# Larger fill transfers, a folded last batch, halved last copies and key transposes by DMA, with a new order, in an attention and gated-convolution kernel

## The chip, the cores and the metric

The kernel runs on one core of one Trainium2 chip. The metric is the device time of one execution in microseconds (us). Before the change it is 197.87 us (median of three runs, 197.86 to 203.43).

TensorE is called PE here, VectorE DVE, ScalarE ACT, GpSimd POOL and SyncE SP, as in the profile. Transfers issued by SP and ACT go by hardware queues ("hardware transfers"), those issued by POOL by the software queue.

## The reference

```python
# q, k, v: (8 batches, 8 heads, 576, 64); p: (8, 8, 32, 64); all float32
p_packed = softmax_attention(p, k, v)            # 32 packed queries per head
a = softmax_attention(q, p_packed, p_packed)     # 576 queries over 32 packed keys
x = a.transpose(0, 2, 1, 3).reshape(8, 576, 512)
x1, x2, x3 = split(x @ w_proj, 3)                # w_proj: (512, 1536)
X2 = rfft(x2, axis=1)
conv = irfft(X2 * rfft(filter, axis=0), axis=1)  # filter: (576, 512)
out = (x1 * conv * x3) @ w_out                   # (8, 576, 512)
```

The Fourier transforms are matrix products with constants: `wc` and `wt` go to the spectrum, `ac` comes back. `filter` is transformed once, in the fill (products `hp`). Per batch, keys and queries are transposed (`kTp`, `qTp`), scored (`s1`, `s2`), and so on to the output products `o`.

## The kernel before

All operations are recorded first, then put in an order by a built-in plan and emitted in that order, engine by engine. Each batch's keys, values and queries come by three software transfers. Cuts are marked with `...`.

```python
# every tile of the working pools; bufs is the number of buffers of a tag
def tile(self, pool, shape, dtype, tag, bufs, name, kind=None):
    t = pool.tile(shape, dtype, tag=tag, name=name, bufs=bufs)
    self.slot[t.tensor.name] = ((tag, bufs), kind) if kind else ((tag, bufs),)
    return t
...
# the plan counts how many buffers of a tag are in use, not which ones
if any(used[tag] + held.get(tag, 0) + n > limit[tag] for tag, n in more.items()):
...
def load(b):
    ...
    qn = sb([P, H, 4 * D], FP16, tag="qn", name=f"qn_b{b}")          # bufs=2
    nc.gpsimd.dma_start(kn[:], ...)
    nc.gpsimd.dma_start(vn[:], ...)
    nc.gpsimd.dma_start(qn[:], ...)
    ...
    if b >= TURNED:                                                    # 4
        nc.sync.dma_start_transpose(qT..., qn...)                      # queries by DMA
...
# the fill
nc.sync.dma_start(ident[:], d_id.ap()[:])
for i in range(4):
    nc.scalar.dma_start(wc[:, i, :], d_wc.ap()[:, i, :])
    nc.sync.dma_start(filt[i][:], fsrc[:, TILE_I[i], :])
nc.scalar.dma_start(wt[:], d_wt.ap()[:])
nc.sync.dma_start(filt[4][0:32, :], ftail[0])
nc.sync.dma_start(filt[4][32:64, :], ftail[1])
load(0)
...                                                                    # wp, three parts
nc.sync.dma_start(ac[:], d_ac.ap()[:])
load(1)
...
# keys, all batches: PE transposes into PSUM, copies by DVE or ACT
nc.tensor.transpose(tp[:, hh, ii, :], kn[:, 2 * g + hh, ts(ii, P)], ident[0:KP, 0:KP])
...
pair, APART = [None], (0, B - 1)      # batches whose inverse products are not folded
...
os_ = sb([P, DM], FP32, tag="os", name=f"os_b{b}", bufs=5)
nc.scalar.mul(out=os_[:], in_=o[:], mul=float(1.0 / SC_Y))
```

The softmax here doesn't subtract the row's maximum and nothing guards it: scores larger than these inputs give would overflow.

## Time and profile before

| | before |
|---|---|
| fast runs / slow runs seen | about 197.8 to 199.8 / 203 to 206 us |
| profiled span | 195.3 us, granted clock 1.00 |
| PE busy | 183.8 us, 94% of the span |
| chain that ended last | PE 87%, DMA 6% |
| first real matmul | 7.77 us |
| last matmul ends | 190.5 us |

PE decides. The fast runs are of two sorts: 197.8 to 198.0 us where the granted clock was 0.999 or 1.00, 198.6 to 199.8 where it was 0.984 to 0.991. "Loss", which the prediction defines, is the time at which a matmul starts less the useful matmul work before it: where loss is flat PE is fed, and each step up is a stop. The lines themselves stand in the prediction.

### The profile page before, as it was taken

How to read it: one execution, taken by the hardware profiler on the slowest of the kernel's cores; microseconds unless marked ns; L12 is line 12 of the kernel's file. 1: busy time of each engine (PE TensorE's matmuls, PEld its weight loads, DVE VectorE, ACT ScalarE, POOL GpSimd, SP SyncE). 2: the span in 40 equal slices, each digit the busy share in tenths (PEclk: the TensorE clock that was granted, in tenths of full speed). 3: DMA queues.
4: the chain of work that ended last, by engine and by line, in shares of the span. 5: the costliest groups of instructions: out<-in, count | busy, mean ns of one | idle time of the engine just before them, and what ended most of it. 6: DMA issues, size and time to landing. Idle time of an engine off the chain costs nothing.

```text
span 195.3 us, 5806 instructions
## 1 busy us (share of the span) xinstructions
PE 183.8 (94%) x2425; PEld 116.2 (59%) x2425; DVE 143.9 (74%) x268; ACT 126.3 (65%) x265; POOL 133.3 (68%) x108
## 2 busy tenths in 40 slices
PE   5949979999999999999999999999999999999990
PEld 4614745676775677656666666667656565664640
DVE  4435575988759987988798699848698897796720
ACT  0634586777998989847686775888667935434241
POOL 7611547697466999679987999399159968963100
PEclk9999999999999999999999999999999999999999
DMA  6999999999999999999999695934012202322335
GB/s 173 242 293 193 206 208 196 197 202 204 191 189 269 202 217 140 112 203 221 141 286 172 148 229 60 203 146 111 0 54 78 90 0 82 138 55 107 110 103 166
DMA packets 44842, 30.95 MB, mean 158 GB/s; under 512 B 16336, under 2 KB 39376, under 8 KB 44816
## 3 DMA queue, kind: packets, MB, share of 16 engines
q0 software_dynamic: 29312, 16.52, 61.2%
q1 hardware_dynamic: 14784, 13.34, 27.4%
q10 hardware_dynamic: 720, 0.72, 1.4%
q8 instruction: 19, 0.31, 0.6%
q14 instruction: 7, 0.06, 0.1%
HBM read 35.55 MB, written 9.44 MB: 230 GB/s over the span
## 4 chain that ended last, share of the span: by engine, by line
PE 87%; DMA 6%; ACT 2%; POOL 1%; issue 1%; DVE 0%; SPq 0%; ACTq 0%
PE x_b L493 31%; PE o_b L493 16%; PE f_b L493 9%; PE fp_b L493 5%; PE s_b L493 5%; PE kTp_b L493 4%; PE qp_b L493 4%; DMA ident<-c_id 3%; PE pv_b L493 3%; PE hp L493 3%; DMA filt<-in_moe_filter_fft_dram 3%; PE a2tp_b L493 2%; PE qTp_b L493 1%; PE fpt_b L493 1%; POOL a_b L493 1%; ACT e_b L493 1%
## 5 line engine op out<-in xcount | busy, mean ns | idle before, releaser
L493 PE MATMUL x_b<-a2t_b,qm_b 128*128 128x64 f16 (+1 forms) x256 | 47.0, 286 | 0.0
L493 POOL TENSOR_TENSOR gm_b<-tt_b,tt_b 128x512 f16<-128x512 f32 (+1 forms) x28 | 39.3, 1427 | 7.3 <-DVE tt_b L493 6.8
L493 DVE TENSOR_TENSOR tt_b<-f_b,h 128x1024 f32<-128x1024 f32 x32 | 38.4, 1218 | 5.5 <-PE f_b L493 5.3
L493 PE MATMUL x_b<-ac,gm_b 128*128 128x64 f16 (+3 forms) x312 | 41.0, 252 | 0.0
L493 PE MATMUL o_b<-wout,y_b 128*128 128x512 f16 x128 | 37.9, 379 | 0.0
L493 POOL TENSOR_TENSOR tt_b<-tt_b,tt_b 128x1024 f32<-128x1024 f32 x12 | 28.3, 2360 | 10.1 <-DVE tt_b L493 9.2
L493 ACT ACTIVATE os_b<-o_b 128x512 f32<-128x512 f32 x36 | 21.3, 598 | 19.6 <-PE o_b L493 18.8
L493 DVE TENSOR_TENSOR w_b<-x1s_b,x_b 128x512 f32<-128x512 f32 (+1 forms) x40 | 24.8, 628 | 8.4 <-ACT x1s_b L493 5.0
L493 PEld LDWEIGHTS <-gm_b 128*128 128x128 f16 x312 | 23.7, 98 | 11.2 <-issue 1.3
L493 ACT COPY x1s_b<-x_b 128x512 f32<-128x512 f32 (+1 forms) x40 | 21.6, 548 | 10.5 <-PE x_b L493 6.0
L493 ACT CAST qm_b<-qp_b 128x512 f16<-128x512 f32 x48 | 26.0, 598 | 2.9 <-PE qp_b L493 1.6
L493 ACT ACTIVATE e_b<-s_b 96x384 f16<-96x384 f32 (+1 forms) x48 | 23.7, 526 | 3.7 <-PE s_b L493 2.6
L493 PE MATMUL f_b<-qm_b,fa_b 128*128 128x512 f16 x80 | 25.9, 380 | 0.0
L493 POOL TENSOR_TENSOR fa_b<-ez_b 128x512 f16<-128x512 f32 x14 | 17.7, 1273 | 9.5 <-ACT ez_b L493 9.5
L493 POOL TENSOR_TENSOR a_b<-e_b,zr_b 128x1152 f16<-128x1152 f16 (+2 forms) x10 | 17.3, 1739 | 9.1 <-DVE zr_b L493 5.1
L493 DVE SCALAR_TENSOR_TENSOR y_b<-w_b,x_b 128x512 f16<-128x512 f32 x32 | 21.1, 683 | 2.6 <-PE x_b L493 2.4
L493 PEld LDWEIGHTS <-qm_b 128*128 128x128 f16 x256 | 18.1, 98 | 8.0 <-issue 0.6
L493 PEld LDWEIGHTS <-a_b 128*128 128x128 f16 x240 | 17.1, 98 | 8.8 <-POOL a_b L493 2.3
L493 PEld LDWEIGHTS <-y_b 128*128 128x128 f16 x128 | 11.3, 98 | 7.8 <-issue 0.2
L493 ACT COPY ez_b<-fp_b 128x512 f32<-128x512 f32 x16 | 9.4, 590 | 8.9 <-PE fp_b L493 4.6
L493 PE MATMUL kTp_b<-ident,kn_b 96*128 96x96 f16 x192 | 14.2, 206 | 0.0
L493 PEld LDWEIGHTS <-kn_b 96*128 96x128 f16 x192 | 11.2, 97 | 2.6 <-issue 0.2
(78 smaller groups left out, 300.5 us busy)
## 6 DMA issues: line engine op xcount, KB each, us to landing
out_dram<-os_b SPq DMA_DIRECT2D x24, 256.0 KB, 2.4
kn_b<-in_k_dram POOLq DMA_DIRECT2D x8, 576.0 KB, 10.8
vn_b<-in_v_dram POOLq DMA_DIRECT2D x8, 576.0 KB, 13.6
qn_b<-in_q_dram POOLq DMA_DIRECT2D x8, 512.0 KB, 12.1
out_dram<-os_b SPq DMA_DIRECT2D x16, 128.0 KB, 2.4
wp<-in_moe_w_proj_dram POOLq DMA_DIRECT2D x3, 512.0 KB, 16.4
filt<-in_moe_filter_fft_dram SPq DMA_DIRECT2D x4, 256.0 KB, 5.5
out_dram<-os_b SPq DMA_DIRECT2D x16, 64.0 KB, 2.3
```

Source lines behind the costliest of these rows:

```text
L493: ins = op.call(*op.args, **op.kw).ins
```

## The change

The intent: take PE work away (keys of batches 6 and 7 transposed by DMA; batch 7 folded), shorten the fill (eight hardware transfers, so that none waits for another), shorten the end (last copies in halves on two engines), and plan the order anew.

```diff
-    kTr = [... for r in range(4)]
+    kTr = [... for r in range(5)]
-    TURNED = 4
+    TURNED, KEYS, NK = (4, 5, 6, 7), (6, 7), 5
...
-    nc.sync.dma_start(ident[:], d_id.ap()[:])
-    for i in range(4):
-        nc.scalar.dma_start(wc[:, i, :], d_wc.ap()[:, i, :])
-        nc.sync.dma_start(filt[i][:], fsrc[:, TILE_I[i], :])
-    nc.scalar.dma_start(wt[:], d_wt.ap()[:])
...
+    half = slice(0, 768), slice(768, 1664)                   # wc with the identity at its end
+    for u in range(2):
+        nc.scalar.dma_start(wci[:, half[u]], d_wc.ap()[:, half[u]])
+        nc.sync.dma_start(filt[:, ts(u, 2 * DM)], fsrc[:, ts(u, 2 * DM)])
+    for u in range(2):
+        nc.scalar.dma_start(wt[64 * u:64 * u + 64, u, :], ...)
+        nc.vector.memset(wt[64 * u:64 * u + 64, 1 - u, :], 0.0)
+        nc.sync.dma_start(ftail[32 * u:32 * u + 32, :], fend[u])
...
-    nc.sync.dma_start(ac[:], d_ac.ap()[:])
+    nc.gpsimd.dma_start(ac..., d_ac...)
...
+        if b in KEYS:
+            for g in range(4):
+                nc.sync.dma_start_transpose(kTr[(4 * b + g) % NK]..., kn[:, 2 * g:2 * g + 2, :]...)
...
+            by = nc.vector if b == 0 else nc.gpsimd          # normalisation of batch 0
...
-    pair, APART = [None], (0, B - 1)
+    APART = (0,)
...
+            if b == B - 1:
+                nc.scalar.mul(out=os_[:, 0:DM // 2], ...)
+                nc.vector.tensor_scalar_mul(out=os_[:, DM // 2:], ...)
...
-PRIORITY = (...)                                             # the order, a packed table
+PRIORITY = (...)
```

Smaller changes are left out here (fewer buffers for `pk` and `zs`, the filter in another tile, the model of transfers inside the plan).

## The prediction

> **What bounds the kernel now.** I read first how busy each engine is in stretches of the span, then the chain that ended last, then the timeline of the fill and of the end, and the groups by shape for durations. Columns of the first view: stretch, its length, then busy microseconds (us) per engine with the number of instructions, granted TensorE clock, DMA share, GB/s.
>
> ```profile
> 0.00:5.00 5.00, 2.88 (x14) 2.08 (x15) 2.28 (x13) 0.01 (x1) 3.94 (x9) 1.00 0.62 174
> 5.00:10.00 5.00, 5.00 (x25) 2.93 (x24) 1.98 (x3) 3.02 (x4) 3.02 (x5) 1.00 1.21 246
> 10.00:15.00 5.00, 2.50 (x12) 0.74 (x11) 1.83 (x4) 1.75 (x4) 0.74 (x1) 1.00 1.18 285
> ...
> 40.00:60.00 20.00, 20.00 (x376) 13.99 (x371) 14.42 (x35) 16.21 (x37) 14.31 (x14) 1.00 1.49 200
> ...
> 120.00:140.00 20.00, 20.00 (x298) 12.98 (x295) 16.15 (x32) 14.91 (x35) 13.97 (x10) 1.00 0.63 125
> ...
> 190.00:195.30 5.30, 0.49 (x3) 0.00 (x0) 0.00 (x0) 0.90 (x2) 0.00 (x0) 1.00 0.60 187
> ```
>
> From 40 us to 190 PE, the first engine, is busy all the time and no other engine is over 93% in any stretch. Before that and after it, it isn't. Busy can hide small gaps, because a 512-column matmul lasts 0.38 us while the next starts after 0.216. So I summed each matmul's issue time instead (columns/2.4 + 2.5 ns, not below 27 ns; the 4- or 8-fold overlapped small ones divided accordingly; fillers named spin count nothing). Call the time minus this useful work done so far the **loss**. In the trace the loss is 7.8 us when the first real matmul starts (7.77), 11.4 at the first key transpose (17.95), 12.7 at 21.8, 14.3 at 25.2, 16.8 at 29.2 and 17.55 at 32.4. From there to the last matmul at 190.5 it grows by only 2.1, nearly all at the changes of tile shape around the qp and pv products. So the kernel is: 17.5 us lost in the fill, 170.6 us of PE work, 2.1 us of switching, 4.8 us after the last matmul.
>
> The chain that ended last (start, length, what) shows what the fill waits for:
>
> ```profile
> 1.20 5.18 DMA filt<-in_moe_filter_fft_dram
> 6.39 0.35 SPq L493
> ...
> 6.78 6.26 DMA ident<-c_id
> 13.04 0.14 issue
> 13.18 0.22 PE pTp_b L493
> 13.39 4.72 PE hp L493 x18
> 18.11 1.02 PE kTp_b L493 x24
> ...
> 185.65 0.69 PE o_b L493 x3
> ```
>
> The identity is the eleventh transfer on the two hardware queues; SP issues it only when an earlier one has landed, because eight are allowed at once (its instruction waits for that count). So no transpose can start before 13.0, and the filter products (hp) come so late that they keep PE till 18. The POOL timeline gives the landings of the other stream, since each issue waits for an earlier transfer:
>
> ```profile
> 12.80 0.74 POOL L493 DMA_DIRECT2D wp<-in_moe_w_proj_dram  x1 [3.91 <-DMA kn_b<-in_k_dram]
> 17.31 0.79 POOL L493 DMA_DIRECT2D kn_b<-in_k_dram  x1 [3.77 <-DMA vn_b<-in_v_dram]
> 19.93 0.63 POOL L493 DMA_DIRECT2D qt_b<-in_q_dram  x1 [1.83 <-DMA qn_b<-in_q_dram]
> ```
>
> Keys at about 12.5, values 17.0, queries 19.6; later landings in the trace are 2.6 to 3.5 us apart. Values took 4.5 us because the constant ac (576 KB) was under way beside them.
>
> **The Trainium skill.** "TensorE: Matmul & The Clock Gate", section "Back-to-back issue gap", gives N/2.4 + 2.5 ns between matmuls at full clock. The trace agrees: 24 key transposes of 96 columns in 1.02 us are 42.5 ns each, the formula says 42.5. "DMA: Bandwidth & Descriptors", "Rules for kernel authors", says to coalesce small transfers into large ones and that issuing from several engines does not add bandwidth, since all use the same 16 DMA engines. The trace agrees with the second part (values slow beside ac) and cannot show the first. The same page, "Latency and other measured facts", gives 261 GB/s for a DMA transpose; here the 512 KB query transposes take 7.2 us from issue to landing, about 73 GB/s, so I use 7.2 and a quarter of the bytes per key piece, about 3 us. None of the pages says when a transfer on a hardware queue is delayed by the software queue.
>
> **Part by part.**
> 1. *Keys of batches 6 and 7.* Removed: 2 x 24 PE transposes at 42.5 ns = 2.04 us, all on the bound engine, plus 4 copies of 644 ns on ACT and 4 of 448 ns on DVE, which lie beside PE. Added: eight transposes on SP's queue. In the new order batch 6's keys can be transposed from 84 us of PE work on and are used at 94; batch 7's between 100 and about 108, used from 113 to 117. There is room, and the DMA share at that stage is low (0.63 and less).
> 2. *Batch 7 folded.* Each of four inverse products has 3 x 512, 2 x 288 and 2 x 224 columns before, 3 x 288 and 3 x 224 after: 3 x 215.8 less 122.5 and 95.8 = 429 ns, four times 1.72 us; the 64-column ones go from 20 to 12, 8 x 29.2 ns = 0.23. Together 1.95 us of PE. Added on POOL: two sums of 2.36 us become two sums and four of 1.27, 5.1 us more, in the last 50 us, where POOL is under half busy.
> 3. *The fill.* Eight hardware transfers, none waiting for another; identity within the first constants; half of wt is cleared on chip and not loaded; ac goes behind the second batch on the software queue. About 1.73 MB must land for the filter products. At the 230 to 250 GB/s of this stage, from about 2 us, that is 9 to 9.5 us, against 12.3 before. The activation table loads at about 2.5 instead of 5.0, since ACT no longer waits to issue. I estimate the first hp at 6.0 (the first half is 0.7 MB), a wait for the second half to about 9.5, and the first key transpose, which comes after 5.67 us of work in the new order, at 12.6: loss 6.9, not 11.4. The rest of the chain added 6.1 us of loss; DVE instead of POOL for batch 0's normalisation takes up to 0.5 off. That makes 12.5 to 13.
>    The other limit is the software stream. With keys at 10.5 and the old distances: values 13.6, queries 16.4, first two parts of wp 19.6 and 22.6, keys of batch 1 25.7, last wp 28.4, values 31.4, queries 34.3, ac 36.6, keys of batch 2 39.5. The new order needs them after 14.9, 17.9, 21.4, 22.9, 24.3 and 28.0 us of work (from keys of batch 1 on), so the loss is at least 10.8, 10.5, 10.0, 11.4, 12.3 and 11.5. Both limits nearly meet; I take 13.2 instead of 17.55: **4.3 us** gained.
> 4. *The end.* Timeline, last line:
>
> ```profile
> 190.57 0.60 ACT L493 ACTIVATE os_b<-o_b 128x512 f32<-128x512 f32 x1 [0.27 <-PE o_b L493]
> ```
>    Halves of 256 columns on ACT and DVE should take about 0.38 us (the 256-column copies here take 381 and 418 ns), so 0.2 us less; one issue beside another on the second queue may give 0.1 more. 0.3 us.
>
> Sum: 2.04 + 1.95 + 4.3 + 0.3 = 8.6 us. I take off 0.8 for new waits, below. 197.87 - 7.8 = 190.1, rounded to 190.0.
>
> **Rivals.**
> - *The folded batch makes POOL the end.* PE has 11.6 us of work between the last spectrum product of batch 7 and its first inverse. POOL needs batch 6's four sums first, then 2 x 2.36 + 4 x 1.27. Reckoned from the spectrum product, the first folded sum has 1 to 2 us of slack and the fourth about none. If POOL or DVE runs late, PE idles 1 to 3 us: 191 to 193. For it: the loss before is flat (19.6) from 155 to 187 us, so nothing hid this; against: the order was made for it.
> - *SP blocks.* Its queue is in order: the transposes of batch 7 wait until the score products of batch 6 have released the key buffers, and five finished output tiles stand behind them. All five buffers are then full, and ACT's next output copy, at 107 us of work, could wait 2 to 3 us for a store to land, stopping ACT. PE's PSUM buffers cover part: 0 to 2 us, 190 to 192.
> - *The fill is limited by bandwidth and hardly moves.* All bytes but 160 KB still come; if larger transfers run no faster and the stream of batch 1 lands only 1.5 us earlier, loss goes to 16: 192.8. Against: ac is out of the way of keys, values and queries.
> - *Fill better than thought:* loss 11.5, 188.4.
>
> **Range and chances.** PE's 4 us are near certain, as PE is the bound for 150 us. The fill gives 2 to 6, new waits take 0 to 3. So 187.6 to 192.8 eight times in ten. 2% is 193.9; missing it needs a poor fill and a late POOL together. Faster 0.94, within 2% 0.05, slower 0.01.
>
> **What would show it.** Identity no longer in the chain; first hp near 6 us, first kTp near 12.6; PE loss near 13 at 33 us and about 15 at the end; PE matmuls 48 + 12 fewer besides spins; kTp x144 instead of x192; x_b at 512 columns from ac x12. Wrong if PE shows gaps over 0.5 us after 33 us, especially before the last inverse products (released by POOL gm_b), or near the SP transposes (ACT os_b released by a DMA), or if keys of batch 0 land no earlier than 12.

## The result

The changed kernel takes **205.61 us** (median of four runs, 204.26 to 206.62), against 200.65 us for the kernel before in the same rounds (197.86 to 203.65). Ratios here are the mean time of one kernel's fast runs over that of the other's of the same rounds, so not quite the ratio of the medians: 1.039, interval 1.028 to 1.049. The prediction said 190.0 and 0.94 for faster. It was slower.

The busy-time view by stretch (length; PE, PE weight load, DVE, ACT, POOL with instruction counts; granted clock; DMA share; GB/s) of the changed kernel:

```profile
5.00:10.00 5.00, 3.89 (x17) 1.62 (x16) 1.90 (x3) 2.27 (x4) 2.36 (x3) 1.00 1.20 279
10.00:15.00 5.00, 4.83 (x38) 2.06 (x37) 3.31 (x8) 2.31 (x5) 2.27 (x3) 1.00 1.41 197
40.00:60.00 20.00, 20.00 (x338) 13.51 (x336) 14.42 (x32) 17.68 (x40) 14.20 (x14) 1.00 1.41 210
60.00:70.00 10.00, 10.00 (x208) 7.62 (x206) 9.29 (x20) 9.33 (x22) 3.48 (x3) 1.00 1.51 214
70.00:80.00 10.00, 0.53 (x9) 0.26 (x5) 1.24 (x3) 0.93 (x3) 1.24 (x2) 0.73 0.81 127
80.00:85.00 5.00, 1.73 (x14) 0.75 (x22) 0.00 (x0) 0.58 (x1) 5.00 (x4) 0.50 0.84 105
85.00:90.00 5.00, 5.00 (x53) 2.58 (x54) 4.33 (x5) 2.93 (x6) 5.00 (x5) 0.68 0.55 105
90.00:95.00 5.00, 5.00 (x121) 3.84 (x118) 4.04 (x6) 3.08 (x7) 5.00 (x4) 1.00 0.01 3
```

The fill is better: PE is busy for 4.83 of the 5 us from 10 to 15, where it had 2.50. Then, from 70 to 80, PE is busy for 0.53 us of 10, and DVE, ACT and POOL for no more than 1.24 each; POOL comes back first, at 78.7. The same view in finer stretches shows a clock of 1.00 up to 74.5, 0.50 from there to 88.2, and 1.00 again after it. "TensorE: Matmul & The Clock Gate" in the Trainium skill, section "What's actually happening", says that the clock drops to half after an idle window of about 3.4 us and comes back after a busy one. The trace agrees: PE's last matmul before the stop ends at 70.5, the clock drops 4.0 us later, and it comes back 4.9 us after PE's restart at 83.3 (the 0.73 and 0.68 above are means over a stretch).

Loss tells how much each cost. It is 15.1 us at 69.4, 28.1 at 83.3 and 30.4 at 90, against 18.3 in the kernel before from 69 to 80. So one stop of 12.9 us and 2.3 us of cold clock lie in these 20 us. From 90 to the last matmul loss grows by only 1.7. Take the 15.2 us away from 205.6 and 190.4 is left, which is about what was predicted; the repaired kernel of experiment 1 will take 1.7 us more than that. The question is what the stop is.

The chain that ended last, for the changed kernel (start, length, what), runs straight through it:

```profile
55.49 17.80 DMA qn_b<-in_q_dram
73.44 4.74 DMA qT_b<-qn_b
...
78.75 0.89 POOL qn_b L509
79.66 2.35 POOL tt_b L509
82.00 1.23 POOL fa_b L509
83.28 0.61 PE f_b L509
```

Before, the chain was PE from 13 us on, but for DVE, ACT and POOL between 23 and 30. Here a load (17.8 us from issue to landing), a DMA transpose, and then three POOL instructions come first. The POOL timeline of the changed kernel says which instruction stood there, and for how long:

```profile
63.14 0.82 POOL L509 DMA_DIRECT2D kn_b<-in_k_dram  x1
78.74 0.89 POOL L509 DMA_DIRECT2D qn_b<-in_q_dram  x1 [14.78 <-DMA qT_b<-qn_b]
79.66 2.35 POOL L509 TENSOR_TENSOR tt_b<-tt_b,tt_b 128x1024 f32<-128x1024 f32 x1
81.96 1.26 POOL L509 TENSOR_TENSOR fa_b<-ez_b 128x512 f16<-128x512 f32 x1
```

And the PE timeline, at the end of its stop:

```profile
83.28 0.61 PE L509 MATMUL f_b<-qm_b,fa_b 128*128 128x512 f16 x1 [12.74 <-POOL fa_b L509]
```

POOL was ready to issue the load of batch 5's queries at 64 us. It waited 14.8 us, until the transpose of batch *4's* queries had landed. The sum `fa` of batch 2, which PE needed at 70.5, stood two instructions behind on the same queue.

In the kernel before, the same load comes after those sums (its issue is at 77.75 us, without a wait):

```profile
74.07 2.52 POOL L493 TENSOR_TENSOR gm_b<-tt_b,tt_b 128x512 f16<-128x512 f32 x2
76.53 1.29 POOL L493 TENSOR_TENSOR fa_b<-ez_b 128x512 f16<-128x512 f32 x1
77.75 0.91 POOL L493 DMA_DIRECT2D qn_b<-in_q_dram  x1
```

Why should loading batch 5 wait for a transpose of batch 4? The addresses of the query tiles in the two built kernels say it. By batch, 0 to 7, the buffer is

```
before   0 1 0 1 0 1 0 1
changed  0 1 0 1 0 0 1 0
```

Batch 5's queries were given the buffer that batch 4's had just been given. Batch 3's buffer was as good as free (in experiment 1 a load into it waits 0.9 us); why the pool did not hand it out was not looked into. The load must therefore wait until batch 4's queries have been loaded *and* read. Of all tiles with two buffers per batch, only the queries have this break in the alternation. The built instruction list of the changed kernel (which could be read before predicting) shows both halves of the trouble:

```
46 kn_b_330 <- in_k_dram                       [waits for a load, PE]
47 qn_b_332 <- in_q_dram                       [waits for DMAHW6 (the transpose), two loads]
48 tt_b_310 <- tt_b_299, tt_b_310
49 fa_b_293 <- ez_b_295
```

### The profile page after: what moved, and what is told of

The parts are those of the page before. It is cut to its first block, busy times and chain, and to the rows that moved or that the text cites.

```text
span 204.0 us, 5677 instructions
## 1 busy us (share of the span) xinstructions
PE 179.8 (88%) x2353; PEld 112.3 (55%) x2353; DVE 145.3 (71%) x272; ACT 122.9 (60%) x261; POOL 137.5 (67%) x111
## 3 DMA queue, kind: packets, MB, share of 16 engines
q1 hardware_dynamic: 18944, 13.70, 28.1%
## 4 chain that ended last, share of the span: by engine, by line
PE 56%; DMA 22%; POOL 12%; DVE 5%; issue 2%; ACT 1%; SPq 1%; POOLq 0%; ACTq 0%
PE x_b L509 19%; PE o_b L509 12%; DMA qn_b<-in_q_dram 9%; DMA vn_b<-in_v_dram 7%; PE f_b L509 6%; DMA ftail<-in_moe_filter_fft_dram 4%; PE fp_b L509 3%; POOL tt_b L509 3%; POOL gm_b L509 3%; POOL fa_b L509 3%; PE hp L509 3%; PE s_b L509 2%; DMA qT_b<-qn_b 2%; PE qp_b L509 2%; PE pv_b L509 2%; DVE tt_b L509 2%
## 5 line engine op out<-in xcount | busy, mean ns | idle before, releaser
L509 PE MATMUL x_b<-a2t_b,qm_b 128*128 128x512 f16 (+1 forms) x256 | 45.4, 287 | 0.6 <-DVE tt_b L509 0.6
L509 POOL TENSOR_TENSOR tt_b<-tt_b,tt_b 128x1024 f32<-128x1024 f32 x14 | 33.0, 2361 | 6.6 <-DVE tt_b L509 6.5
L509 PE MATMUL f_b<-qm_b,fa_b 128*128 128x512 f16 x80 | 25.9, 392 | 12.7 <-POOL fa_b L509 12.7
L509 PE MATMUL x_b<-ac,gm_b 128*128 128x64 f16 (+3 forms) x300 | 35.8, 252 | 0.4 <-DVE y_b L509 0.2
L509 PE MATMUL o_b<-wout,y_b 128*128 128x512 f16 x128 | 35.8, 379 | 0.0
L509 ACT ACTIVATE os_b<-o_b 128x512 f32<-128x512 f32 (+1 forms) x36 | 20.2, 570 | 12.4 <-PE o_b L509 11.4
L509 PEld LDWEIGHTS <-qm_b 128*128 128x128 f16 x256 | 17.8, 98 | 10.1 <-issue 1.1
L509 POOL TENSOR_TENSOR fa_b<-ez_b 128x512 f16<-128x512 f32 x15 | 19.0, 1277 | 4.0 <-ACT ez_b L509 3.9
L509 POOL DMA_DIRECT2D qn_b<-in_q_dram x8 | 7.3, 912 | 16.7 <-DMA qT_b<-qn_b 14.8
L509 POOL TENSOR_TENSOR a_b<-e_b,zr_b 128x1152 f16<-128x1152 f16 x7 | 14.9, 2127 | 3.4 <-DVE zr_b L509 3.4
L509 PEld LDWEIGHTS <-fa_b 128*128 128x128 f16 x80 | 7.0, 99 | 16.8 <-POOL fa_b L509 13.4
L509 DVE COPY kT<-kTp_b 128x576 f16<-128x576 f16 x12 | 5.3, 446 | 14.2 <-PE kTp_b L509 14.2
```

The lines of the kernel that those rows point to most:

```text
L509: ins = op.call(*op.args, **op.kw).ins
```

## The experiments

The theory: the buffer choice makes the load wait; the wait is harmful because POOL's queue is in order and urgent sums stand behind it. The rivals: the software stream is late anyway; the key transposes or the folded sums do it; late queries are what hurts. All kernels below give correct results. Times are medians, with the range of fast runs where it matters; the kernel before had fast runs of 197.8 to 199.8 and slow ones of 203.2 to 206.1 in the same rounds.

### 1. Only the buffers of the queries

```diff
 def tile(self, pool, shape, dtype, tag, bufs, name, kind=None):
-    t = pool.tile(shape, dtype, tag=tag, name=name, bufs=bufs)
+    side = {'qn_b%d' % b: b % 2 for b in range(8)}.get(name)
+    t = pool.tile(shape, dtype, tag=tag if side is None else f'qn{side}', name=name,
+                  bufs=bufs if side is None else 1)
```

> The changed kernel with one difference: the eight query tiles alternate between two fixed buffers by batch number (0 1 0 1 0 1 0 1), where its own allocator gave 0 1 0 1 0 0 1 0. The order of instructions on every engine is the same; only the load of batch 5's queries loses its wait for batch 4's query transpose (it waits for batch 3's readers instead) and batch 6's load gets that wait. Theory (the buffer choice made the load wait 14.8 us on POOL's queue, and the sums behind it starved PE for 12.9 us and let its clock drop): POOL's wait before that load under 0.5 us, no PE gap over 1 us at 70 us, granted clock 1.0, time 190.3, between 189 and 191.5. Rival A (the software stream of loads is late anyway, batch 4's queries landing at 73.3): PE stops elsewhere between 70 and 90 us and the time stays above 195. Rival B (key transposes on SP, or the folded sums on POOL): within 1 us of the changed kernel, 204 to 206.

Measured: **192.09 us** (191.25 to 192.54, six runs, all fast; ratio to before 0.965). The instruction order on every engine is identical to the changed kernel's. The POOL timeline of this kernel:

```profile
64.80 0.89 POOL L510 DMA_DIRECT2D qn_b<-in_q_dram  x1 [0.87 <-PE fpt_b L510]
65.72 2.38 POOL L510 TENSOR_TENSOR tt_b<-tt_b,tt_b 128x1024 f32<-128x1024 f32 x1
68.04 1.27 POOL L510 TENSOR_TENSOR fa_b<-ez_b 128x512 f16<-128x512 f32 x1
```

and its busy time by stretch:

```profile
70.00:80.00 10.00, 9.44 (x131) 6.08 (x129) 8.87 (x14) 7.06 (x15) 10.00 (x8) 1.00 1.46 156
80.00:85.00 5.00, 5.00 (x101) 3.48 (x99) 3.41 (x6) 3.71 (x7) 4.09 (x4) 1.00 1.07 156
```

The sum now ends at 69.3 instead of 83.2, PE keeps going and its clock stays full. 13.5 us hang on which of two free-looking buffers a tile got. Rivals A and B fall: everything that they accuse is still in this kernel, and batch 4's queries land even later (75.0 instead of 73.3). It misses my expected 189 to 191.5 by 0.6, taken up below, and POOL still waits 0.87 us before the load, where I expected under 0.5. A second set on another chip gave 192.37:

> The kernel with alternating query buffers once more, as the base of the three that run beside it on the same chip: 191.3 to 192.6 as before.

### 2. The bad buffers kept, the load moved back

```diff
+        load = next(o for o in order if o.dma() and o.out.tensor.name.startswith("qn_b5"))
+        after = next(o for o in order if o.engine == "POOL" and o.out.tensor.name.startswith("a2_b3"))
+        order.remove(load)
+        order.insert(order.index(after) + 1, load)
```

> The changed kernel with its bad buffer sequence kept (batch 5's queries in batch 4's buffer), but the load of batch 5's queries moved six instructions later on POOL, behind the normalisation product of batch 3. Theory (the harm is not that the queries come late, it is that POOL's queue is in order and the waiting load stood before sums that PE needed): by then only 1 to 4 us of wait are left, nothing urgent stands behind it, time 190 to 192.5. Rival (batch 5's queries come too late for their consumer, whatever stands behind the load): 200 or more, as in the changed kernel.

Measured: **192.38 us** (192.00 to 193.43). The load went past eight instructions (the expectation says six), and no wait is left by then. It is issued at 78.39 in this kernel's POOL timeline, within 0.4 us of the changed kernel's 78.74:

```profile
76.32 2.12 POOL L515 TENSOR_TENSOR a_b<-e_b,zr_b 128x1152 f16<-128x1152 f16 x1
78.39 0.94 POOL L515 DMA_DIRECT2D qn_b<-in_q_dram  x1
```

So batch 5's queries come just as late as in the slow kernel (landing at 84.5 and 84.6), and it costs nothing. What cost 13 us was the place of a waiting instruction in an in-order queue. Either repair is enough: the right buffer or the later place.

### 3. The two ingredients put into the kernel before

Both kernels move the load of batch 5's queries directly behind the load of batch 5's keys. One has the bad buffers as well, the other the alternating ones.

```diff
-        return self.schedule()[1]
+        order = self.schedule()[1]
+        ...            # as in 2, with "kn_b5" in place of "a2_b3"
+    side = dict(zip(['qn_b%d' % b for b in range(8)], (0, 1, 0, 1, 0, 0, 1, 0))).get(name)   # bad
+    side = {'qn_b%d' % b: b % 2 for b in range(8)}.get(name)                                   # good
```

Bad buffers:

> The kernel before with the two ingredients put in by hand and nothing else of the change: batch 5's queries in batch 4's buffer, and their load moved up on POOL to directly behind the load of batch 5's keys, before the sums. Theory: POOL waits from 67.9 to about 77 us for the query transpose of batch 4, the sum of batch 2 that PE needs comes 9 us late, PE stops for 7 to 9 us and its clock drops for some us after: 204 to 209. Rival (something else in the new kernel makes the stop): within 1 us of the kernel before.

Good buffers:

> The kernel before with the load of batch 5's queries moved up in the same way but with the good, alternating buffers. Theory: the early issue alone costs nothing, since batch 3's buffer is free by then: within 1 us of the kernel before (197 to 199 in its fast state). Rival (an early query load takes bandwidth or POOL time that others need): 1 to 4 us slower.

Measured: bad **210.1 to 212.0 us** in fast runs (ratio 1.059), good **199.3 to 199.7** in fast runs (ratio 1.002, interval 0.997 to 1.007). The bad one was a little slower than the 204 to 209 that I expected. The wait is of the same kind as in the changed kernel, 9.2 us on POOL and, by its waits view, 9.7 us on PE for the sums and differences (`gm`) behind it:

```profile
84.67 0.89 POOL L499 DMA_DIRECT2D qn_b<-in_q_dram  x1 [9.19 <-DMA qT_b<-qn_b]
```

Nothing else of the change is in that kernel. Each ingredient alone is harmless (the early load with good buffers here and in experiment 1, the bad buffers with a late load in experiment 2), both together cost 11.7 us here (means of fast runs, 210.8 against 199.1) and 13.5 in the changed kernel.

### 4. What each part of the change is worth

With the buffers repaired, each part can be undone by itself. My first three tries let the built-in plan make a new order for each kernel, and that spoiled two of them.

```diff
-    APART = (0,)                                              # e6_nofold
+    APART = (0, B - 1)
-    TURNED, KEYS, NK = (4, 5, 6, 7), (6, 7), 5                # e7_nokeys
+    TURNED, KEYS, NK = (4, 5, 6, 7), (), 5
+    # e8_oldfill: wc, filt in four pieces each, identity apart, whole wt, ac on SP
```

> The alternating-buffer kernel with batch 7 not folded (its inverse products and sums as in the kernel before). Theory (PE is the bound there, the sums on POOL are hidden): useful PE work up by 1.95 us and the time up by about the same, 1.5 to 2.4 us over the base. Rival (the folded sums on POOL cost PE waits that ate part of the gain): 0 to 1 us over the base.

> The alternating-buffer kernel with the keys of batches 6 and 7 transposed on PE again, nothing by DMA. Theory: useful PE work up by 2.04 us and the time by 1.5 to 2.4 us. Rival (in the base the loss of PE grows by 1.25 us from 107 to 138 us, where the key transposes run on the sync engine's queue, and by only 0.4 in the kernel before; the transposes cost part of what they save): the loss no longer grows there and the time is only 0.5 to 1.2 us over the base.

> The alternating-buffer kernel with the old fill: thirteen hardware transfers in small pieces, the identity alone as the eleventh, all of wt loaded, the constant ac on the hardware queue; the order after the fill is planned anew for it. Theory (the new fill is worth the 4.3 us that I reckoned, less about 1 that it fell short): loss of PE at 38 us of 17 to 19 instead of 14.7, the granted clock dips in the fill in some runs, the time 2.5 to 4.5 us over the base. Rival (the fill is bound by bytes): within 1 us of the base.

Measured: 193.06, 200.73 and 218.36 us (for the last only one run of six was fast, 210.81). In the second, loss rises by 3.5 us in the last 20 us of the span, far from the keys; in the third it rises again and again after the fill. These are costs of the orders, not of the parts, so they settle nothing.

Then I fixed the emitted order of experiment 1 on every engine and exchanged only the instructions concerned, in place. In the built programs PE differs only in these (not at all for the two fill kernels).

> The alternating-buffer kernel (192.1 and 192.4 in two sets) with batch 7 not folded, and this time its emitted order held fixed on every engine, with only the products and sums concerned exchanged in place. Theory: useful PE work 1.95 us more, time up by 1.7 to 2.2, since nothing else moves; the 0.7 us of the earlier try came from its new order. Rival (the folded sums on POOL cost PE about 1.2 us of waits): up by 0.5 to 1 us again.

> The alternating-buffer kernel, order held fixed, with the keys of batches 6 and 7 transposed on PE (48 transposes and eight copies put in front of their score products, the eight transposes on the sync engine's queue gone). Theory: useful PE work 2.04 us more, but the two waits of PE at 117 us (1.05 us for a key transpose to land) and 131 us (0.6 us for output stores held up on that queue) go, so the time rises by only 0.4 to 1.0 us. Rival (those waits have other causes): up by 1.8 to 2.3 us. The 8.4 us of the earlier try came from its own order.

> The alternating-buffer kernel, order held fixed on PE, with the transfers of the old fill: thirteen small ones, identity as the eleventh, ac on the hardware queue. Theory: loss of PE at 38 us of 17 to 19 instead of 14.8 us, time up by 2.5 to 4.5 us in fast runs. Rival (bound by bytes): within 1 us.

> The alternating-buffer kernel, order held fixed, with only the constant ac moved back from behind the second batch on the software queue to the hardware queue, early. Theory (ac takes bandwidth from values and queries of batch 0): these land 1 to 2 us later and the time rises by 0.5 to 2 us. Rival (there is bandwidth to spare): within 0.4 us, or even faster, since the second batch then lands earlier.

| undone | median | mean of fast runs | over 192.15 | reckoned |
|---|---|---|---|---|
| batch 7 folded | 194.20 | 194.16 | +2.0 | 1.95 |
| keys by DMA | 195.44 | 195.44 | +3.3 | 2.04 |
| new fill | 198.87 | 195.06 | +2.9 | 4.3 |
| only ac put back | 192.18 | 192.20 | +0.05 | part of the 4.3 |

192.15 is the mean of the two sets of experiment 1. It did not run on the chip of these four, where the kernel before was about 0.6 us faster than in the other sets (fast runs 198.53 against 199.1 and 199.2). If each time is taken relative to the kernel before of its own set, the four differences are 2.6, 3.9, 3.0 and 0.7 us, so differences of half a microsecond mean nothing here.

The fold is worth about what was reckoned. The keys are worth more, not less, although one wait that I expected from them is there. It shows in the PE timeline of the second set of experiment 1, where PE waits for a key transpose:

```profile
118.29 0.23 PE L510 MATMUL s_b<-pk,kT 128*128 128x64 f16 x2 [0.89 <-DMA kT<-kn_b]
```

Back on PE, this wait goes, but two steps of loss come in its place (0.4 us each at 110.2 and 134.2, next to the transposes), and the work is longer. The profiled run of that kernel, the slowest of its six, also lost 1.3 us more in the fill; why is open, and of the 3.3 us I count 2 as shown.

The old fill costs 2.9 us in the mean of its three fast runs. One of these (196.22, the profiled one) had a clock of 0.50 from 13.1 to 16.5 us; the other two, at 0.999, are 2.3 us over the base. The old fill also brings back slow runs: four of its seven took 198.9 to 200.5 at a granted clock of 0.96 to 0.97. All twelve runs of experiment 1 had a clock of 0.992 or more. Those four are not in the 2.9.

Moving ac back changed the time by less than can be told here (0.05 or 0.7 us), so my 0.5 to 2 us is neither shown nor ruled out. The first half of that expectation did come true. This is the POOL timeline with ac on the hardware queue; keys of batch 0 landed at 14.4, where they land at 12.5 in experiment 1:

```profile
14.70 0.81 POOL L495 DMA_DIRECT2D kn_b<-in_k_dram  x1 [2.84 <-DMA kn_b<-in_k_dram]
```

Values landed at 17.6 instead of 15.7 and queries at 20.4 instead of 18.5, so all three 1.9 us later. Loss at 25 us is 1.5 us higher than in experiment 1, but at 38 us only about half a microsecond. The profiled run counts as slow (194.6 us); it stopped 2.3 us for a key transpose at 120, the wait shown above.

## Why the prediction was wrong

**The step that failed** is the one that wrote "I take off 0.8 for new waits", with its rivals. Of the four rivals none was the one that came. I asked which engines and queues would be *busier*: POOL at the end, SP's queue. I did not ask, for each load that moved ahead in the new order, what its buffer had to wait for, nor what stood behind it. The new order moved the load of batch 5's queries ahead of sums that PE needed. With the buffer of batch 3 that is harmless, with the buffer of batch 4 it was worth 12.9 us of stop and 2.3 us of cold clock. The list of instructions with their waits, which could be read before the prediction, had it.

**The PE work** was right. Useful work until the last matmul is 166.65 us against 170.64, 3.99 us less, 2.04 + 1.95. This only says that the right matmuls went, since both come from one formula; the measured support is that undoing the fold costs 2.0 us and undoing the keys 3.3. One sum of the prediction does not hold: the `qp` products overlap eightfold (two groups of eight start 0.20 us apart at 60.2 us in the kernel before), and counted so PE has 166.3 us of work, not 170.6, and loss after the fill grows by 6.1 us, not 2.1. So some 4 us that the prediction calls work are time around these products. Differences between the kernels stay within 0.2 us of what is said here, but for the cold clock, which becomes 2.8 instead of 2.3.

**The fill** was mis-sized. Loss at its end is 14.75 us (in the changed kernel and in experiment 1 alike), not 13.2, from 17.5: 2.8 gained, not 4.3, and putting the old fill back costs about as much, 2.3 to 2.9. Three lines of the changed kernel, the first from PE, the second from POOL, the third from PE:

```profile
6.75 0.90 PE L509 MATMUL hp<-fh,wc 128*128 128x512 f16 x3 [0.79 <-ACT fh L509]
12.83 0.81 POOL L509 DMA_DIRECT2D kn_b<-in_k_dram  x1 [1.16 <-DMA kn_b<-in_k_dram]
14.07 1.23 PE L509 MATMUL kTp_b<-wc,kn_b 96*128 96x96 f16 x24
```

The first limit was roughly right: first hp at 6.75 (reckoned 6.0), first kTp at 14.1 with a loss of 8.4 (12.6 and 6.9). The second limit had a wrong premise: keys of batch 0 landed at 12.55, where they landed before (12.51), not at 10.5. The reckoning gave the whole 230 to 250 GB/s to the constants and the filter, while the software stream ran beside them. Values landed at 15.7 and queries at 18.5, 1.1 to 1.3 us earlier than before but some 2 us later than I had them. My own test, "wrong if keys of batch 0 land no earlier than 12", came true. That ac slows this stream, as I argued, is borne out (1.9 us on keys, values and queries when it is put back), but not that much time hangs on it. And the identity, by the order of issue in the trace, was the twelfth hardware transfer, not the eleventh; the reading (eight are out by 2.1 us, the ninth goes at 4.63 when the first has landed at 4.61) stays.

**The end** had the wrong sign. From the end of the last matmul to the end of the span are 5.2 to 5.3 us instead of 4.9. The two halves of the last copy do not run side by side: in the built program the DVE half waits for the ACT half of its tile. In experiment 1:

```profile
185.01 0.38 ACT L510 ACTIVATE os_b<-o_b 128x256 f32<-128x256 f32 x1 [0.26 <-PE o_b L510]
185.43 0.42 DVE L510 TENSOR_SCALAR os_b<-o_b 128x256 f32<-128x256 f32 x1 [0.22 <-ACT os_b L510]
```

So the copy takes 0.84 us where one engine took 0.60, and the last store is issued 1.5 us after the last matmul's end instead of 1.05. That is about the 0.4 us. No run without this wait was made.

**Small waits.** In experiment 1, loss grows from 14.8 to 18.1 in one profile and from 15.1 to 18.7 in the other, so by 3.3 to 3.7 us, where I had 2.1 + 0.8. Three stops make the difference: 0.5 to 0.7 at 71 us (not POOL's `fa`, which is done at 69.3 to 69.5; where the profile names a releaser it is ACT's copy of keys), 0.4 to 1.1 at 117 (key transposes), 0.5 at 131, which was the rival "SP blocks" in small: ACT waits for an output buffer whose store stands on SP's queue. The ACT timeline of the second set of experiment 1 has it:

```profile
131.45 0.60 ACT L510 ACTIVATE os_b<-o_b 128x512 f32<-128x512 f32 x1 [0.28 <-DMA out_dram<-os_b]
```

A key transpose takes 7.4 and 6.7 us, median, from issue to landing in the two profiles (4.7 in the changed kernel), where I reckoned 3. I had also read the wrong stretch: the "DMA share 0.63" is that of 120 to 140 us, while the key transposes of batch 6 fall into 97 to 116 us; from 100 to 120 the share was 0.89 before and is 1.43 in experiment 1.

The rival of POOL at the end did not come: loss is flat from 148 us on.

In sum, for the kernel with the repaired buffers, whose profiled run took 191.98 us against 197.46 for that of before: PE work -3.99, loss -1.6 (reckoned -3.5), end +0.4 (reckoned -0.3), time outside the span -0.3 (not reckoned). That is -5.5 us, where I reckoned -7.8. My 190.0 would have been 2 us too low, but inside its range of 187.6 to 192.8. The changed kernel itself lies outside it by 13 us, for one buffer.

The best kernel is the one of experiment 1: 192.1 to 192.4 us against about 199 for the fast runs of before, or 197.8 for those at full clock.

## What to carry to other kernels

When a change makes a new order, go through the loads that moved ahead and ask for each: which buffer does it write, who reads that buffer last, and which urgent instruction stands behind the load on its engine's queue. A count of free buffers doesn't answer this; the addresses and waits of the built kernel do. If two buffers must alternate, pin them, and don't put a load that may wait in front of compute that others need.

## What the Trainium skill lacked or had wrong

- No page that I found draws from the order of an engine's queue what a *waiting transfer issue* does to the compute instructions behind it. Here it cost POOL 14.8 us and PE 12.7 us, and with the load eight instructions later nothing. "DMA: Bandwidth & Descriptors", section "Rules for kernel authors", would be a place for it.
- No page that I found warns that a pool may hand out the buffer that was handed out last, while the other is as good as free: 0 1 0 1 0 0 1 0 instead of an alternation, worth 13.5 us.
- No page that I found puts a figure on how much a transfer on a hardware queue delays the software stream. Here 576 KB (ac) at 5.3 us made keys, values and queries land 1.9 us later each.
- "DMA: Bandwidth & Descriptors", section "Latency and other measured facts", gives 261 GB/s for a DMA transpose. Here 512 KB took 4.7 us (the one in the chain above) or 7.2 us (median of the kernel before) from issue to landing, so 112 or 73 GB/s; in experiment 1 it took 11.9 us (median), and key pieces of 144 KB took 4.7 to 7.4 us (medians).
- "TensorE: Matmul & The Clock Gate", section "What's actually happening", puts the penalty of the clock's ramp at under 1% of a typical span. Here the kernel before takes 197.8 us at clock 1.00 or 203.5 at 0.96, 2.9% apart. In the slow profile of the first old-fill kernel the clock is 0.50 from 20 to 25 us, so in the fill; with only the old fill exchanged, in place, four of seven runs fell to 0.96 to 0.97, and none of the twelve runs of experiment 1 fell that low. Which wait of the fill decides it was not tested.
